# Attention and two feed-forward layers: the late gate written back to PSUM, its split finished by VectorE, a second buffer for two combinations, new scheduler numbers

## Chip, cores and metric

The kernel runs on one core of one Trainium2 chip. The metric is the device time of one execution in microseconds (us); the time of record is the median of several runs.

## What is computed

```python
attn_out = _attn_ref(q, k, v)          # 4 batches, 8 heads, 576 tokens, head 64, mask in blocks of 64
x = attn_out.transpose(0, 2, 1, 3).reshape(B * S, H * D)      # 2304 x 512
h = x @ moe_w_in                       # 512 -> 2048
x = (np.maximum(h, 0) + alpha * np.minimum(h, 0)) @ moe_w_out # layer 0
h = x @ moe2_w_in
out = (h / (1 + np.exp(-1.702 * h))) @ moe2_w_out             # layer 1
```

Inputs of the attention are fp32, the feed-forward weights are float64 and are narrowed to fp32 on the chip. The matmuls are done in fp32r: each operand is split into a high and a low part, and a product is three matmuls (high by high, high by low, low by high).

## The kernel before

**Early stage.** Attention runs over 20 passes (batch, head pair): transposes on TensorE, scores, softmax on ScalarE and VectorE, a DMA transpose of the split probabilities, and the product with v. Beside it, TensorE computes layer 0 for the first 8 of the 16 slices of 128 hidden units: `gemm1` (line 206) multiplies a block of 288 tokens with eight slices, `gate` makes g from it, `gate_split` splits g into the two parts in `gs`, and `g2_half` (lines 249 to 251) multiplies with the output weights and leaves a partial sum in DRAM (`xa`).

**Late stage.** What is left of layer 0 (8 slices) and all of layer 1 (16 slices) is done in 60 *jobs*. A job is two slices for one *unit* of 512 tokens (the last unit of a layer has 256). Its first product uses one level of Strassen's scheme: seven products of combinations of weights (`ws`) and of x (`xc`), in `first_half` (four of them, 24 matmuls of 128x256, or 18 for the small unit) and `second_half` (18, or 6). They go into two PSUM banks, `ga` and `ep`; there are four such banks, so job p + 2 takes the banks of job p. Between the halves `snap` copies parts out (ScalarE, GpSimd), and `sums` adds them in VectorE (lines 786 to 791), after which the two banks hold h of the two slices. Units run in the order 0, 1, 4, 2, 3 for layer 0 and 0 to 4 for layer 1, with four jobs each in layer 0 and eight in layer 1.

Then, for each of the two banks, `gate` (lines 215 to 224) applies the gate: ScalarE reads the bank into an SBUF tile `g` (two buffers), VectorE multiplies `g` with the bank and writes `g` again; the bank is free after that. `gate_split` (lines 226 to 234) copies `g` on ScalarE to the high part `gh` in fp32r, and GpSimd subtracts, `gl = g - gh` (line 127). Both parts lie in `gs`, which has room for two jobs. `g2` (line 813) multiplies them with the output weights into four accumulator banks `acc`, 24 matmuls of 512 columns for a job (12 for layer 1's small unit). After a unit's last job `block_out` drains the accumulators: in layer 0 it loads the partial sum (`o<-xa`, line 822, two `o` buffers), VectorE adds the accumulator (line 823) and a DMA stores it.

Weights of the late stage are loaded as float64 (`rw`), narrowed by ScalarE and three VectorE operations (lines 154 to 160), and then either combined and stored to DRAM (`comb`, `wc<-wc`) or split at once (`split_w`, VectorE and GpSimd in turn, line 127). `load_x` loads a unit's x (`xr`, 1 MB, one buffer) and `comb_x` makes its seven combinations `xc`, each with one buffer.

**The order of the work** is set by a planner that runs while the kernel is built. Each step is announced with `at(kind, n, fn)`; a step's due number is n plus a tenth of `ORDER[kind]` plus `SHIFT[kind]`. `arrange` then simulates the five queues with the durations of `cost` and the dependences, takes on each engine the ready instruction with the smallest due number, and fixes that order. Each engine executes its list strictly in that order.

Of the kernel before, what the change touches and what calls it, by code (L numbers as in the profile page):

```python
# [10 lines left out]
F32R = mybir.dt.float32r  # L11
# [5 lines left out]
ALU = mybir.AluOpType  # L17
# [28 lines left out]
    "split x 2": 8, "load w": 9, "load w 2": 9, "load x": 9, "load k": 9.5, "load q": 9.5, "load v": 9.5, "load alpha": 9.6,  # L46
}
SHIFT = {
    "comb 2": 94.3, "comb 3": -127.7, "first": -19.1, "gate": -18.1, "gate 2": 14.5, "gemm1": -26.2,
    "gemm1 2": 12.5, "gemm2": 168.7, "half": 66.6, "half out": 34.0, "high": 61.0, "load alpha": -77.9,  # L50
    "load k": 64.3, "load q": -45.2, "load v": 58.7, "load w": 60.2, "load w 2": -69.5, "load w 3": -51.5,
    "load wc": -44.3, "load x": -39.6, "narrow": 188.9, "narrow 2": 43.0, "narrow 3": -38.3, "norm": -13.7,
    "out": 35.0, "prep out": 51.5, "prep t": -194.0, "prep v": 152.1, "pv": -88.9, "pv out": 17.0,
    "rest": 55.6, "score": -123.6, "second": 32.2, "setup": 61.8, "snap": -44.3, "soft": -0.0,
    "split g": 101.8, "split g 2": -42.6, "split w": 8.2, "split w 2": 13.0, "split w 3": -12.4,
    "split x": 384.6, "split x 2": 178.0, "sums": 55.9, "warm": 90.0,
}
BIG = 1.0e30

# [2 lines left out]
def kernel(  # L62
# [19 lines left out]
    NA = 8  # L82
# [9 lines left out]
    TH = TB // 2  # L92
    scale = 1.0 / float(D) ** 0.5

    pe, dve, act, pool, sp = nc.tensor, nc.vector, nc.scalar, nc.gpsimd, nc.sync
# [3 lines left out]
    wts_a = ctx.enter_context(tc.tile_pool(name="wts_a", bufs=1))  # L99
    raw = ctx.enter_context(tc.tile_pool(name="raw", bufs=2))  # L100
    blk = ctx.enter_context(tc.tile_pool(name="blk", bufs=1))
# [11 lines left out]
    nalph = const.tile([128, NF], F32, name="nalph")  # L113
# [5 lines left out]
    def at(kind, n, fn):  # L119
        plan.append((n, ORDER[kind], len(plan), fn, n + 0.1 * ORDER[kind] + SHIFT.get(kind, 0)))  # L120


    def hi_part(dst, src, scale_=1.0):
        act.activation(out=dst, in_=src, func=ACTF.Copy, scale=scale_)  # L124

    def lo_part(eng, dst, src, hi):
        eng.tensor_tensor(out=dst, in0=src, in1=hi.bitcast(F32), op=ALU.subtract)  # L127
# [52 lines left out]
    pend = {}  # L180
    late = {}
# [28 lines left out]
    def gbuf(key, name):  # L210
        if key[0] == 0:
            return tmp_p.tile([128, TA], F32, tag="g", name=name)
        return late["x"].tile([128, TB], F32, tag="g", bufs=2, name=name)

    def gate(key, layer, f):
        ps, n = pend[key, f]
        g = gbuf(key, "g")[:, 0:n]
        if layer == 0:
            act.activation(out=g, in_=ps, func=ACTF.Relu, scale=-1.0)
            dve.scalar_tensor_tensor(out=g, in0=g, scalar=nalph[:, f:f + 1], in1=ps, op0=ALU.mult, op1=ALU.add)  # L220
        else:
            act.activation(out=g, in_=ps, func=ACTF.Sigmoid, scale=1.702)
            dve.tensor_tensor(out=g, in0=g, in1=ps, op=ALU.mult)  # L223
        pend[key, f] = (g, n)

    def gate_split(key, f, lo, z=None):
        g, n = pend.pop((key, f))

        w, z = (TA, f % NA) if key[0] == 0 else (TB, z)
        gh, gl = gs_[:, 2 * z * w:2 * z * w + n], gs_[:, (2 * z + 1) * w:(2 * z + 1) * w + n]  # L230
        hi_part(gh, g)
        lo_part(lo, gl, g, gh)
        gt[key, f] = (gh, gl)
# [59 lines left out]
    hl = [[one.tile([128, 128 * g[3]], F16, name=f"hl{j}{x}") for x in range(NHL[j])] for j, g in enumerate(GRP)]  # L293
# [109 lines left out]
    first = []  # L403
# [136 lines left out]
    for u, (i, g, s) in enumerate(slots):  # L540
        n = 2 * u
# [12 lines left out]
    for i in range(len(passes)):  # L554
# [8 lines left out]
        for z, what in enumerate(todo):  # L563
            n = n0 + z * (cnt - (i == N0)) // len(todo)
# [112 lines left out]
    def load_wc(p):  # L677
        l, (_, t0, n, _), j = jobs[p]
        if l == 0 and j in wc0:
            wc[p] = wc0[j]  # L680
            return
        ts = []
        for i in range(7):
            if n == TB or i in (2, 3, 5, 6):
                t = slot(j if l == 0 else (p - P2) % NSL, i)
                sp.dma_start(out=t.bitcast(F32).rearrange("p h c -> p (h c)"), in_=wcs[l][j][i])
            else:
                t = None
            ts.append(t)
        wc[p] = ts  # L690
        if l == 0:
            wc0[j] = ts

    wc0 = {}
    wc = {}
    UO = (0, 1, 4, 2, 3), (0, 1, 2, 3, 4)
    units = [(l, TB * y, min(TB, NT - TB * y), (l + 1, y)) for l in range(2) for y in UO[l]]
    jobs = [(u[0], u, j) for u in units for j in range(NPAIR[u[0]])]
    xc = {}
# [9 lines left out]
    def comb_x(u, i):  # L709
        l, t0, n, key = u  # L710
        r = xb[key]
        b11, b21 = r[:, 0:2, 0:TH], r[:, 2:4, 0:TH]
        if n < TB:
            x = {0: b11, 1: b21}[i]
        else:
            b12, b22 = r[:, 0:2, TH:TB], r[:, 2:4, TH:TB]
            two_ = {0: (b11, b22, ALU.add), 2: (b12, b22, ALU.subtract), 3: (b21, b11, ALU.subtract), 5: (b11, b12, ALU.add),
                    6: (b21, b22, ALU.add)}
            if i in two_:
                x = late["x"].tile([128, 2, TH], F32, tag="xt", bufs=2, name="xt")  # L720
                y, y2, op = two_[i]
                pool.tensor_tensor(out=x, in0=y, in1=y2, op=op)
            else:
                x = b11 if i == 1 else b22
        pl, tag = (blk, ("xlb", "xh0")[i]) if i < 2 else (late["x"], f"xc{i}")
        t = pl.tile([128, 2, 2, TH], F32R, tag=tag, name="xc")
        hi_part(t[:, 0], x)
        lo_part(dve, t[:, 1], x, t[:, 0])
        xc[key, i] = t

    def prod(ps, p, i, y, first, last):
        key = jobs[p][1][3]
        w, x = wc[p][i], xc[key, y]
        z = 0
        for c in range(2):
            sl = slice(128 * c, 128 * c + 128)
            for st_, mv in ((w[:, 0, sl], x[:, 0, c]), (w[:, 0, sl], x[:, 1, c]), (w[:, 1, sl], x[:, 0, c])):
                pe.matmul(ps, st_, mv, start=first and z == 0, stop=last and z == 5, skip_group_check=True)  # L738
                z += 1

# [30 lines left out]
    def second_half(p):  # L771
        g, e = mm[p][:2]
        if jobs[p][1][2] == TB:
            prod(g[:, 0:TH], p, 6, 6, False, False)
            prod(g[:, TH:TB], p, 4, 4, False, True)
            prod(e[:, 0:TH], p, 3, 3, False, True)
        else:
            prod(g[:, 0:TH], p, 6, 1, False, True)
        wc.pop(p)
# [53 lines left out]
    n = n2  # L833
# [6 lines left out]
    for p, (l, u, j) in enumerate(jobs):  # L840
        n, key = place[p], u[3]
        at("load wc", place[max(p - 2, 0)] - 4 * (p < 2), lambda p=p: load_wc(p))
        at("first", n, lambda p=p: first_half(p))
        at("snap", n + 0.3, lambda p=p: snap(p))
        at("second", n + 0.9, lambda p=p: second_half(p))
        at("sums", n + 1.3, lambda p=p: sums(p))
        for y, f in enumerate(fpair(l, j)):
            z = 2 * (p % 2) + y
            at("gate 2", n + 1.4, lambda key=key, l=l, f=f: gate(key, l, f))
            at("split g 2", n + 1.4, lambda key=key, f=f, z=z: gate_split(key, f, pool, z))  # L850
            at("gemm2", place[p + 2] + 0.1 + 0.1 * y, lambda u=u, f=f, a=j == 0 and y == 0, b=j == NPAIR[l] - 1 and y == 1: g2(u, f, a, b))
        if j == NPAIR[l] - 1:
            at("out", place[p + 2] + 0.4, lambda u=u: block_out(u))
    for u in units:
        n = start[u[3]]
# [11 lines left out]
    for y, (n, l, j, f) in enumerate(sorted(seq_w, key=lambda o: o[0])):  # L867
        n = at_w = max(int(n), at_w + 1)
# [74 lines left out]
def cost(eng, kind, ins, outs):  # L943

    n = max(free_size(a) for a in ins + outs)
    psum = any(a.tensor.space == PSUM for a in ins)
    if eng == "PE":
        mv, w = ins[:2]
        cols, load = free_size(outs[0]) * (2 if mv.dtype == F32 else 1), free_size(w)
        rows = list(w.ap)[0][1]  # L950
        time = cols / 2.4 + (13.3 if mv.dtype == F32R else 2.7)
        return time, load / 1.2 + 2.5 if BYTES[w.dtype] == 4 else load / 4.8, cols * rows / 128, mode(w)
    if eng == "Activation":
        return (50 if psum else 93) + n / 1.2 + (187 if len(outs) > 1 else 0),
    full = sum(free_size(a) == n for a in ins)
    if eng == "Pool":
        return (35 + n / 1.2 if not ins else 244 + n / 1.2 if full < 2 else 148 + 2.1 * n),
    if not ins:
        return (40 if outs[0].tensor.space == PSUM else 7) + n / 1.92,
    if psum and len(ins) < 3 or n < 8 or kind == "InstTensorReduce":  # L960
        return (65 if n < 8 else 155) + n / 0.96,
    if full < 2:
        return 64 + n / 1.92,
    return (129 if len(ins) > 2 else 68) + n / 0.96,
# [174 lines left out]
```

## Time and profile before

| | |
|---|---|
| median of 3 runs | 1079.42 us (1077.47 to 1079.83) |
| the profiled execution | 1076.91 us, span of its instructions 1075.1 us |
| TensorE matmul busy, weight load busy | 1003.6 us, 895.2 us |
| VectorE, ScalarE, GpSimd busy | 720.8, 630.2, 521.3 us |
| mean granted TensorE clock | 0.981 of full speed |

The matmuls of a profile are pipelined: a record lasts longer than the distance to the next one, so that busy time is no measure of how near TensorE is to its peak; the distance between starts, and the idle time of the weight loader (PEld), tell more.

### The profile page before, as it was taken

Reading aid. Unit: us, or ns where it says so; the run is one execution under the profiler, and the core shown is the slowest. Engines: PE = TensorE matmul, PEld = TensorE weight load, DVE = VectorE, ACT = ScalarE, POOL = GpSimd, SP = SyncE. Lnnn points to the kernel's source line nnn. Section 1 sums busy time; section 2 is a strip of 40 time slices with the busy share of each in tenths; the row PEclk is TensorE's granted clock in tenths of the full one; section 3 lists DMA queues with packets and bytes.
Section 4 is the critical chain, followed back from the end, with each engine's and each line's share of the span. In section 5 each row is a group of like instructions: output and inputs, shape, how many; then the busy total and the mean of one; then the engine's idle time right before and its main releaser. Section 6 shows DMA issues by size and latency. Waiting matters only on the chain.

```text
span 1075.1 us, 19697 instructions
## 1 busy us (share of the span) xinstructions
PE 1003.6 (93%) x6934; PEld 895.2 (83%) x6934; DVE 720.8 (67%) x1314; ACT 630.2 (59%) x1492; POOL 521.3 (48%) x505
## 2 busy tenths in 40 slices
PE   6777979999999999899997999899999999999998
PEld 3545868889889888899987998788889988989887
DVE  6987999888988875879876878588934324422211
ACT  5777988888888885555544544455434333433332
POOL 3344443433425254578656776555555544434322
PEclk9898989999999999999999999999999999999999
DMA  7899999999998979772645688977585666564340
GB/s 177 203 207 202 193 208 209 207 210 194 227 203 168 197 171 256 263 261 98 224 149 187 194 302 281 306 255 267 169 286 185 221 198 186 187 201 122 118 157 20
DMA packets 308082, 216.92 MB, mean 202 GB/s; under 512 B 219664, under 2 KB 246288, under 8 KB 307984
## 3 DMA queue, kind: packets, MB, share of 16 engines
q1 hardware_dynamic: 307984, 215.67, 73.6%
q8 instruction: 55, 0.90, 0.4%
q14 instruction: 43, 0.35, 0.1%
HBM read 143.27 MB, written 40.89 MB: 171 GB/s over the span
## 4 chain that ended last, share of the span: by engine, by line
PE 59%; DMA 11%; ACT 10%; DVE 7%; issue 3%; POOL 2%; SPq 1%; ACTq 0%; DVEq 0%; POOLq 0%
PE acc L813 20%; PE ga L738 13%; PE ep L738 9%; PE pv L523 4%; PE h L206 4%; ACT e L468 2%; DMA rw<-in_moe_w_out_dram 2%; PE sc L445 2%; PE x L250 2%; PE x L249 2%; PE x L251 2%; ACT hl L488 2%; DMA pt<-hl 2%; DMA wc<-wc 2%; DMA rw<-in_moe_w_in_dram 2%
## 5 line engine op out<-in xcount | busy, mean ns | idle before, releaser
L127 POOL TENSOR_TENSOR gs<-g,gs 128x512 fp32r<-128x512 f32 (+2 forms) x184 | 206.3, 1126 | 242.1 <-ACT gs L124 218.7
L738 PE MATMUL ga<-xc,ws 128*128 128x256 f32 x1368 | 189.2, 284 | 10.9 <-DVE g L223 10.7
L738 PEld LDWEIGHTS ga<-xc,ws 128*128 128x128 f32 x1368 | 178.2, 191 | 21.6 <-DVE g L223 13.9
L813 PE MATMUL acc<-wh,gs 128*128 128x512 f32 x576 | 182.4, 392 | 0.5 <-DVE o L823 0.5
L124 ACT ACTIVATE gs<-g 128x512 fp32r<-128x512 f32 (+2 forms) x184 | 97.8, 536 | 81.9 <-PE acc L813 60.3
L738 PE MATMUL ep<-xc,ws 128*128 128x256 f32 x936 | 134.4, 287 | 2.4 <-DVE g L220 1.5
L738 PEld LDWEIGHTS ep<-xc,ws 128*128 128x128 f32 x936 | 124.9, 194 | 7.2 <-DVE g L220 1.9
L813 PEld LDWEIGHTS acc<-wh,gs 128*128 128x128 f32 x576 | 106.4, 188 | 20.3 <-DVE o L823 0.9
L813 PE MATMUL acc<-wl,gs 128*128 128x512 f32 x288 | 112.7, 391 | 0.0
L523 PE MATMUL pv<-pt,vp 128*128 128x256 f16 (+2 forms) x960 | 92.7, 244 | 9.1 <-DMA pt<-hl 5.5
L813 PE MATMUL acc<-gs,wh 128*128 128x512 f32 (+1 forms) x320 | 94.6, 376 | 4.7 <-DVE o L823 4.6
L498 DVE SCALAR_TENSOR_TENSOR hl<-e,stat,hl 64x64 f16<-64x64 f32 (+4 forms) x160 | 94.9, 623 | 5.1 <-ACT hl L488 2.7
L206 PE MATMUL h<-xh,wh 128*128 128x288 f32 x256 | 80.3, 314 | 11.2 <-DVE g L220 4.4
L488 ACT ACTIVATE hl<-e,stat 64x64 f16<-64x64 f32 (+4 forms) x160 | 79.4, 552 | 10.5 <-DVE stat L478 6.4
L468 ACT ACTIVATE e<-sc,stat 64x64 f32<-64x64 f32 (+4 forms) x160 | 82.9, 520 | 4.2 <-DVE stat L460 3.5
L523 PEld LDWEIGHTS <-vp 128*128 128x128 bf16 x960 | 64.6, 100 | 23.4 <-DMA pt<-hl 9.6
L206 PE MATMUL h<-xlb,wh 128*128 128x288 f32 x256 | 77.9, 304 | 2.5 <-POOL xlb L127 2.4
L249 PE MATMUL x<-gs,wh 128*128 128x288 f32 x256 | 76.6, 303 | 1.0 <-ACT wh L124 0.6
L250 PE MATMUL x<-gs,wh 128*128 128x288 f32 x256 | 76.2, 299 | 0.4 <-POOL gs L127 0.4
L206 PE MATMUL h<-xh,wl 128*128 128x288 f32 x256 | 76.3, 299 | 0.0
L251 PE MATMUL x<-gs,wl 128*128 128x288 f32 x256 | 76.2, 301 | 0.0
L764 POOL TENSOR_TENSOR v<-u,v 128x256 f32<-128x256 f32 x48 | 40.9, 852 | 66.2 <-ACT v L763 66.1
(94 smaller groups left out, 2165.0 us busy)
## 6 DMA issues: line engine op xcount, KB each, us to landing
ws<-wc SPq DMA_DIRECT2D x284, 256.0 KB, 3.8
wc<-wc SPq DMA_DIRECT2D x84, 256.0 KB, 2.6
rw<-in_moe_w_in_dram SPq DMA_DIRECT2D x32, 512.0 KB, 4.7
rw<-in_moe_w_out_dram SPq DMA_DIRECT2D x32, 512.0 KB, 4.3
nat_q<-in_q_dram SPq DMA_DIRECT2D x24, 288.0 KB, 4.3
nat_k<-in_k_dram SPq DMA_DIRECT2D x16, 288.0 KB, 3.9
nat_v<-in_v_dram SPq DMA_DIRECT2D x16, 288.0 KB, 4.2
xa<-xo SPq DMA_DIRECT2D x32, 144.0 KB, 2.8
```

Source lines behind the costliest of these rows:

```text
L124: act.activation(out=dst, in_=src, func=ACTF.Copy, scale=scale_)
L127: eng.tensor_tensor(out=dst, in0=src, in1=hi.bitcast(F32), op=ALU.subtract)
L206: pe.matmul(ps, st_[:, sl], mv[:, c], start=z == 0, stop=z == 3 * KD - 1)
L249: pe.matmul(ps, oh[:, sl], gh, start=f == 0, stop=False)
L250: pe.matmul(ps, oh[:, sl], gl, start=False, stop=False)
L251: pe.matmul(ps, ol[:, sl], gh, start=False, stop=f == NA - 1)
L468: act.activation(out=eo, in_=v[:, h] if len(heads) > 1 else v, func=ACTF.Exp, scale=-1.0, bias=stat[0:m, 0, a:a + 1], accum_out=stat[0:m, ...
L488: act.activation(out=o, in_=e, func=ACTF.Copy, scale=r)
L498: dve.scalar_tensor_tensor(out=hl_part(j, 1, m, nk, h), in0=es[h][0:m, off:off + nk], scalar=stat[0:m, 2, 2 * a + h:2 * a + h + 1], in1=hl ...
L523: pe.matmul(o, l, r, start=z == 0, stop=z == len(ops) - 1)
L738: pe.matmul(ps, st_, mv, start=first and z == 0, stop=last and z == 5, skip_group_check=True)
L813: pe.matmul(ps, a, b_, start=first and z == 0, stop=last and z == 2)
```

## The change

Four edits.

1. In the late stage (`key[0]` is not 0), `gate` writes its result into the PSUM bank in place of `g`. The high part is then copied from the bank by ScalarE, and the low part is subtracted from there by VectorE in place of GpSimd (`split g 2` now names `dve`).
2. For every second unit, combinations 0 and 2 of x get a tile of their own: combination 0 in a tile `xc0`, combination 2 in two tiles that held the weight slice 7 of the early stage. A combination is now handled as a pair of views.
3. `SHIFT` has new numbers for nearly every kind.
4. The planner's cost of a ScalarE operation with SBUF input and a second tensor operand rises from 93 to 186 ns plus the columns.

```diff
 SHIFT = {
-    "comb 2": 94.3, "comb 3": -127.7, "first": -19.1, "gate": -18.1, "gate 2": 14.5, "gemm1": -26.2,
...
+    "comb 2": 35.0, "comb 3": -62.2, "first": 58.5, "gate": -35.3, "gate 2": 49.1, "gemm1": 46.5,
...
     def gate(key, layer, f):
         ps, n = pend[key, f]
         g = gbuf(key, "g")[:, 0:n]
+        to = ps if key[0] else g
         if layer == 0:
             act.activation(out=g, in_=ps, func=ACTF.Relu, scale=-1.0)
-            dve.scalar_tensor_tensor(out=g, in0=g, scalar=nalph[:, f:f + 1], in1=ps, op0=ALU.mult, op1=ALU.add)
+            dve.scalar_tensor_tensor(out=to, in0=g, scalar=nalph[:, f:f + 1], in1=ps, op0=ALU.mult, op1=ALU.add)
         else:
             act.activation(out=g, in_=ps, func=ACTF.Sigmoid, scale=1.702)
-            dve.tensor_tensor(out=g, in0=g, in1=ps, op=ALU.mult)
-        pend[key, f] = (g, n)
+            dve.tensor_tensor(out=to, in0=g, in1=ps, op=ALU.mult)
+        pend[key, f] = (to, n)
...
-        pl, tag = (blk, ("xlb", "xh0")[i]) if i < 2 else (late["x"], f"xc{i}")
-        t = pl.tile([128, 2, 2, TH], F32R, tag=tag, name="xc")
-        hi_part(t[:, 0], x)
-        lo_part(dve, t[:, 1], x, t[:, 0])
+        odd = units.index(u) % 2
+        if i == 2 and odd:
+            t = [wts_a.tile([128, 2, TH], F32R, tag=f"{y}0_{NA - 1}", name="xc") for y in "hl"]
+        else:
+            pl, tag = (blk, ("xlb", "xh0")[i]) if i < 2 and not (odd and i == 0) else (late["x"], f"xc{i}")
+            t = pl.tile([128, 2, 2, TH], F32R, tag=tag, name="xc")
+            t = t[:, 0], t[:, 1]
+        hi_part(t[0], x)
+        lo_part(dve, t[1], x, t[0])
...
-            at("split g 2", n + 1.4, lambda key=key, f=f, z=z: gate_split(key, f, pool, z))
+            at("split g 2", n + 1.4, lambda key=key, f=f, z=z: gate_split(key, f, dve, z))
...
-        return (50 if psum else 93) + n / 1.2 + (187 if len(outs) > 1 else 0),
+        return (50 if psum else 93 if len(ins) < 2 else 186) + n / 1.2 + (187 if len(outs) > 1 else 0),
```

The new numbers move the work. Three places follow.

TensorE in the first jobs of layer 1's second unit. `ga` and `ep` rows are products of jobs (42 to a job), `acc` rows are `g2`. Before:

```order
L813 MATMUL acc<-wh_9498,gs 128x512
L738 MATMUL ga<-xc,ws 128x256 x12
L738 MATMUL ep<-xc,ws 128x256 x12
L738 MATMUL ga<-xc,ws 128x256 x12
L738 MATMUL ep<-xc,ws 128x256 x5
L738 MATMUL ga<-xc,ws 128x256 x12
L738 MATMUL ep<-xc,ws 128x256 x13
L738 MATMUL ga<-xc,ws 128x256 x12
L738 MATMUL ep<-xc,ws 128x256 x6
L813 MATMUL acc<-wh_8260,gs 128x512
```

The same place now:

```order
L819 MATMUL acc<-wh_9501,gs 128x512
L744 MATMUL ga<-xc,ws 128x256 x12
L744 MATMUL ep<-xc,ws 128x256 x6
L744 MATMUL ga<-xc,ws 128x256 x12
L744 MATMUL ep<-xc,ws 128x256 x12
L819 MATMUL acc<-wh_8262,gs 128x512
```

Before, two whole jobs (84 products) stood between two stretches of `g2`, here jobs 30 and 31; now it is the second half of one job and the first half of the next (42), then the 24 matmuls of `g2`, and so on in the same pattern through nearly the whole late stage.

VectorE in the first eight jobs of layer 1, over one job. Lines 157 to 160 narrow a weight tile, `wl` is a weight's low part, 786 to 789 (792 to 795 now) are the sums, 223 (224 now) the gate. Before:

```order
L786 TENSOR_TENSOR u<-ep,v 128x256
L157 TENSOR_SCALAR wa<-sq 128x512
L787 TENSOR_TENSOR u<-u,ga 128x256
L159 SCALAR_TENSOR_TENSOR wa<-sq,wa 128x512
L788 TENSOR_TENSOR ep<-ep,u 128x256
L160 SCALAR_TENSOR_TENSOR sq<-rw,wa 128x512
L157 TENSOR_SCALAR wa<-sq 128x512
L223 TENSOR_TENSOR g<-g,ga 128x512
L159 SCALAR_TENSOR_TENSOR wa<-sq,wa 128x512
L127 TENSOR_TENSOR wl_9119<-sq,wh_9118 128x512
L160 SCALAR_TENSOR_TENSOR sq<-rw,wa 128x512
L223 TENSOR_TENSOR g<-g,ep 128x512
```

Now:

```order
L160 SCALAR_TENSOR_TENSOR sq<-rw,wa 128x512
L793 TENSOR_TENSOR u<-u,ga 128x256
L794 TENSOR_TENSOR ep<-ep,u 128x256
L795 TENSOR_TENSOR ga<-ga,u 128x256
L127 TENSOR_TENSOR wl_9122<-sq,wh_9121 128x512
L157 TENSOR_SCALAR wa<-sq 128x512
L224 TENSOR_TENSOR ga<-g,ga 128x512
L159 SCALAR_TENSOR_TENSOR wa<-sq,wa 128x512
L224 TENSOR_TENSOR ep<-g,ep 128x512
L127 TENSOR_TENSOR gs<-ga,gs 128x512
L160 SCALAR_TENSOR_TENSOR sq<-rw,wa 128x512
L127 TENSOR_TENSOR gs<-ep,gs 128x512
```

The sums stand together, the gate writes `ga` and `ep`, and the two low parts `gs` have come to VectorE.

The DMA queue at the turn from layer 0's unit 4 to unit 2. Before:

```order
L824 DMA x2s<-o 128x512 x2
L822 DMA o<-xa 128x512
L653 DMA wc_4_0_134<-wc 128x512
L704 DMA xr<-xs 128x4x512
L822 DMA o<-xa 128x512
L653 DMA wc_4_1_135<-wc 128x512
```

Now:

```order
L830 DMA x2s<-o 128x512 x2
L828 DMA o<-xa 128x512
L141 DMA rw<-in_moe_w_in_dram 128x4x128
L828 DMA o<-xa 128x512
L654 DMA wc_4_0_134<-wc 128x512
L141 DMA rw<-in_moe_w_in_dram 128x4x128
L654 DMA wc_4_1_135<-wc 128x512
L830 DMA x2s<-o 128x512 x2
L654 DMA wc_4_2_136<-wc 128x512
L828 DMA o<-xa 128x256
L654 DMA wc_4_3_137<-wc 128x512
L705 DMA xr<-xs 128x4x512
```

The 1 MB load of the next x (`xr`) stood between the third and the fourth partial sum of the unit that is drained; now it follows both, and a weight load of 512 KB stands between them.

## Rows read from the trace of the kernel before

**Rows 1.** The page, part 1: busy time, share of the span, instructions.
```profile
PE 1003.6 (93%) x6934; PEld 895.2 (83%) x6934; DVE 720.8 (67%) x1314; ACT 630.2 (59%) x1492; POOL 521.3 (48%) x505
```
**Rows 2.** Busy time by stretch: us, then each engine, granted clock, DMA share, GB/s.
```profile
0.00:200.00 200.00, 162.46 (x1181) 128.76 (x1182) 169.47 (x342) 157.55 (x413) 80.44 (x82) 0.93 0.95 202
...
455.00:690.00 235.00, 226.46 (x1496) 208.32 (x1495) 179.62 (x274) 119.72 (x250) 163.73 (x157) 0.99 0.65 217
690.00:790.00 100.00, 91.52 (x546) 80.37 (x545) 75.65 (x109) 48.89 (x90) 57.27 (x48) 0.98 0.76 258
```
**Rows 3.** The same view in stretches of 25 us, those with a lowered clock.
```profile
575.00:600.00 25.00, 20.39 (x157) 20.09 (x156) 14.90 (x25) 10.04 (x23) 16.00 (x19) 0.93 0.46 156
...
675.00:700.00 25.00, 21.79 (x132) 19.28 (x132) 13.91 (x30) 11.78 (x24) 14.51 (x17) 0.93 0.86 284
...
775.00:800.00 25.00, 23.10 (x162) 21.98 (x161) 10.72 (x26) 10.08 (x19) 11.94 (x13) 0.93 0.97 340
```
**Rows 4.** The chain that ended last: start, us, what.
```profile
840.48 2.88 PE ga L738 x24
...
845.51 5.47 PE acc L813 x24
...
870.92 0.64 ACT gs L124
...
871.63 1.30 POOL gs L127
...
1058.84 12.73 PE acc L813 x56
```
**Rows 5.** Waits of the weight loader, 650 to 800 us: total, times, longest.
```profile
PEld ga L738 <- DVE g L223: 12.2, 7, 2.3
...
PEld ep L738 <- DVE g L220: 0.7, 1, 0.7
```
**Rows 6.** The same, 455 to 650 us.
```profile
PEld acc L813 <- DVE o L823: 4.8, 1, 4.8
PEld ep L738 <- DVE g L220: 1.2, 1, 1.2
```
**Rows 7.** The same, 400 to 455 us.
```profile
PEld h L206 <- DVE g L220: 2.4, 1, 2.4
```
**Rows 8.** The same, 800 to 1075 us.
```profile
PEld ga L738 <- DVE g L223: 1.8, 3, 1.4
```
**Rows 9.** Timeline around 755 us: start, us, engine, line, operation.
```profile
751.66 1.29 POOL L127 TENSOR_TENSOR gs<-g,gs 128x512 fp32r<-128x512 f32 x1 [2.99 <-ACT gs L124]
751.77 1.73 DVE L159 SCALAR_TENSOR_TENSOR wa<-sq,wa 128x512 int32<-128x512 int32 x1
...
755.45 0.41 DVE L789 TENSOR_TENSOR ga<-ga,u 128x256 f32<-128x256 f32 x1
...
755.89 0.69 DVE L127 TENSOR_TENSOR wl<-sq,wh 128x512 fp32r<-128x512 f32 x1
...
756.59 0.69 DVE L223 TENSOR_TENSOR g<-g,ga 128x512 f32<-128x512 f32 x1
```
**Rows 10.** Groups by line, 690 to 775 us: busy, mean ns, idle before.
```profile
L159 DVE SCALAR_TENSOR_TENSOR wa<-sq,wa 128x512 int32<-128x512 int32 x13 | 16.3, 1254 | 0.0
L127 POOL TENSOR_TENSOR gs<-g,gs 128x512 fp32r<-128x512 f32 x14 | 20.5, 1474 | 16.1 <-ACT gs L124 16.1
L154 ACT ACTIVATE sq<-rw 128x512 f32<-128x512 f32 x13 | 8.5, 663 | 14.0 <-DMA rw<-in_moe_w_out_dram 14.0
```
**Rows 11.** Timeline at the turn of a unit.
```profile
570.77 0.37 SPq L704 DMA_DIRECT2D xr<-xs  x1
571.23 0.64 SPq L822 DMA_DIRECT2D o<-xa  x1
...
580.55 0.69 DVE L823 TENSOR_TENSOR o<-acc,o 128x512 f32<-128x512 f32 x1 [3.97 <-DMA o<-xa]
```
**Rows 12.** Waits over the whole span.
```profile
ACT g L222 <- POOL gs L127: 69.3, 54, 2.5
```

More of the change, by code (lines that the diff above doesn't have):

```diff
@@ L48 @@
 SHIFT = {
-    "comb 2": 94.3, "comb 3": -127.7, "first": -19.1, "gate": -18.1, "gate 2": 14.5, "gemm1": -26.2,
[L50 to L56, printed above, removed]
+    "comb 2": 35.0, "comb 3": -62.2, "first": 58.5, "gate": -35.3, "gate 2": 49.1, "gemm1": 46.5,
+    "gemm1 2": 12.5, "gemm2": 59.1, "half": 110.6, "half out": -22.5, "high": 19.0, "load alpha": -0.4,
+    "load k": 9.7, "load q": -168.0, "load v": -25.2, "load w": 61.9, "load w 2": 11.9, "load w 3": 3.0,
+    "load wc": -24.2, "load x": -20.5, "narrow": 297.4, "narrow 2": 65.6, "narrow 3": 20.9, "norm": 13.4,
+    "out": 4.8, "prep out": 20.2, "prep t": -7.1, "prep v": 81.6, "pv": 5.9, "pv out": 23.1, "rest": 20.2,
+    "score": -5.4, "second": 58.6, "setup": -9.8, "snap": -57.0, "soft": -4.0, "split g": 64.1,
+    "split g 2": -56.1, "split w": -8.4, "split w 2": 13.3, "split w 3": -3.0, "split x": 56.6,
+    "split x 2": 192.1, "sums": -166.0, "warm": 67.8,
 }
@@ L736, in prod @@
             sl = slice(128 * c, 128 * c + 128)
-            for st_, mv in ((w[:, 0, sl], x[:, 0, c]), (w[:, 0, sl], x[:, 1, c]), (w[:, 1, sl], x[:, 0, c])):
+            for st_, mv in ((w[:, 0, sl], x[0][:, c]), (w[:, 0, sl], x[1][:, c]), (w[:, 1, sl], x[0][:, c])):
                 pe.matmul(ps, st_, mv, start=first and z == 0, stop=last and z == 5, skip_group_check=True)
```

## The prediction

> **What bounds the kernel now.** I read the totals first, then busy time by stretch, the chain, the waits of the weight loader, and last the timeline at the worst waits. The totals say TensorE: 1003.6 us of 1075.1 with a matmul running, no other engine above 67% [rows 1]. The matmuls are the same 6934 after the change, so time can only come from the distance between them. Where nothing holds it, TensorE goes at a fixed pace: 24 products in 2.88 us (0.12 each), 24 matmuls of the second layer in 5.47 us (0.228 each) [rows 4]. So I look for what TensorE loses. In the first 200 us it is busy for only 162 of them, but there the DMA engines are at 0.95 [rows 2]. The change adds no work there and the order of TensorE's list is nearly the same, so this part is not where I expect a result. In the late stage the loss is in few places:
>
> - After 650 us the weight loader waits 12.2 us in 7 waits for the gate's multiplication, the one that frees a product bank, and 0.7 us for the same thing in layer 0 [rows 5].
> - At the turn of a unit it waits 4.8 us once for VectorE's drain of an accumulator, and 1.2 us for a gate [rows 6].
> - Before the late stage it waits 2.4 us for an early gate [rows 7], and after 800 us only 1.8 us in three waits [rows 8].
> - Three stretches of 25 us have a mean granted clock of 0.93 [rows 3]. Each follows one of these waits, and 7% of 25 us is about 1.75 us of work lost.
>
> **Why the gate is late.** ScalarE waits 69.3 us in all, in 54 waits, for GpSimd's low part before it may overwrite `g` [rows 12], and its list is stuck for that time. In the chain GpSimd's low part takes 1.30 us after a high part of 0.64 [rows 4]. VectorE, which must do the gate, has in 690 to 790 us 75.65 us of work [rows 2], but part of it is stretched: the narrowing operation of line 159 took 1.73 us when it began just behind a low part of GpSimd, while a VectorE subtraction of the same size with both inputs in SBUF took 0.69 a little later [rows 9]. The mean of line 159 there is 1.254 us [rows 10].
>
> **The change part by part.**
>
> *Low part to VectorE.* GpSimd loses 120 operations of about 1.3 us; VectorE gains 120 with one operand in PSUM. The nearest row is the gate's multiplication, also one PSUM and one SBUF operand of 512 columns: 0.69 us [rows 9]. In 690 to 775 us that is 14 x 0.69 = 9.7 us more for VectorE [rows 10]. Against it, what GpSimd's low parts stretched goes: line 159 alone has 13 x (1.254 - 0.69) = 7.3 us of stretch, and line 160 is alike. GpSimd keeps other work, so I count half of about 15 us. VectorE's load so rises by about 2 us in 100: the cover is a VectorE that stays below 80% busy. If the stretch stays, it is 85%.
>
> The Trainium skill ("VectorE: DVE Perf Modes", Rules for kernel authors) says that matmul output which is worked on several times should be copied from PSUM to SBUF first, and its errata section gives a PSUM source 62 cycles more at 0.96 GHz, about 0.065 us as an estimate, which would make the 28 gate and split operations of that stretch 1.8 us dearer; the rows show 0.69 us with PSUM and 0.69 us without [rows 9], so I give it no price.
>
> *The bank is held longer.* It is now free after the low part, not after the multiplication: one more ScalarE copy (0.64 [rows 4]) and one more subtraction (0.69), with hand-overs about 1.5 us. Who waits for it is the first half of the job after next. Here the new order matters. Before, jobs 30 and 31 stood together, which left 6 matmuls of the second layer and 42 products between a job's end and the reuse of its bank: 1.4 + 5.0 = 6.4 us. Now 24 and 42 stand there: 10.5 us, almost everywhere. The chain to be covered is four sums of 0.41, sigmoid, multiplication, copy and subtraction of about 0.65 to 0.69 each, and one more 0.69 for the second bank: 5.0 us with nothing else in VectorE's list. In layer 1's first eight jobs two weight tiles are narrowed per job, six operations and a low part in the same list: 7 x 0.69 makes 9.8 us, still covered. So I let 10 of the 12.9 + 2 x 1.75 = 16.4 us of gate waits and slow clock go (bounds: none, all). What is late next there is the narrowed weight: ScalarE already waits 14.0 us for the float64 loads [rows 10], which nothing in the change shortens.
>
> *DMA order at the unit turn.* The 1 MB load was issued at 570.77, the partial sum right behind it at 571.23, and its adder ran only at 580.55, after 3.97 us of idle VectorE [rows 11]; that is the 4.8 us wait. Now the two partial sums go first, with one 512 KB weight load between. I take 6 of 4.8 + 1.2 + 1.75 = 7.75 us off (bounds: none, all).
>
> *Early end and steady part.* The last early blocks are put in another order on TensorE, which may or may not keep their one wait [rows 7]: 1.5 of 2.4 us (0 to 2.4). After 800 us: 1 of 1.8 us.
>
> *Two combinations with a second buffer.* They lift a wait of ScalarE and GpSimd at ten unit turns. The previous unit's products of combinations 0 and 2 come first in its last job, some 9 us before the next unit begins, so that wait is hidden and the edit is worth nothing by itself; without that cover it would cost one copy and one subtraction per turn, 1.3 us.
>
> *New costs.* The last 56 matmuls of the second layer hid all of the last gates, 12.73 us [rows 4]; now 24 stand behind the last product, 12 of them (2.7 us) in front of the ones that need the last gate, whose chain is about 2.4 us for 256 columns: 0.5 us (0 to 1.5). VectorE's more crowded list in 455 to 690 us, where it has 179.6 of 235 us [rows 2] and gets 42 low parts, 27 us at most: +3 us for new short waits (0 to 10). The planner's numbers and the ScalarE cost line also move things in the attention stage, by a few places: 0, between -6 and +6.
>
> **Sum.** -10 - 6 - 1.5 - 1 + 0.5 + 3 = -15 us. The profiled execution took 1076.9 us, 2.5 below the median of 1079.4; against the median this gives 1064 us.
>
> **Rivals.**
>
> - *The bank becomes the bound (slower).* If VectorE's narrowing operations stay at 1.25 us, the covered chain in layer 1's first eight jobs is 5.0 + 6 x 1.25 + 0.7 = 13 us, over the 10.5 that the order leaves. That is the point from which it decides. Then each of the 8 + 1 + 3 gate waits after 455 us [rows 5, 6, 8] grows by the 1.5 us of longer holding: +18, less 6.5 for the unit turn: 1091 us. For it: 0.93 clocks show how thin the cover is; against it: the operation that stretched them leaves GpSimd. Chance 0.10.
> - *The stretch after 650 us is bound by its loads.* The DMA share is 0.86 in 675 to 700 us [rows 3], ScalarE waits for float64 words, and the gate sits behind them in ScalarE's list. Then the 10 us stay, the rest comes: 1074 us. Chance 0.20.
> - *Everything late goes.* All waits and slow clocks, 16.4 + 7.75 + 2.4 + 1.8 = 28 us, and no new ones: 1051 us, and below if the attention stage gains too. Chance 0.10.
> - *Nothing moves.* The new numbers move the 1 MB load and the waits elsewhere at the same price (the turn's and the gates' waits stay, 2.5 gained, 3.5 lost): 1080 us. Chance 0.08.
>
> **Chances and range.** The forecast, with 1056 to 1071 us around it, keeps 0.52. A measurement of this kernel tells about 0.2% (2.2 us) from no change. Faster: 0.52 + 0.20 + 0.10 = 0.82; within: 0.08; slower: 0.10. The range goes from 1050 to 1078 us: below it is half of the case in which everything goes, above it the slower case and part of no change.
>
> **What would show it.** Right: ScalarE's wait for GpSimd's low part (69.3 us) is gone; the low part runs on VectorE in about 0.69 us; line 159's mean falls below 1.0 us; the waits of `ga` for VectorE after 650 us fall from 12.2 us to some 4, now named by the low part; the accumulator wait of 4.8 us is gone and with it one slow clock. Wrong: `ga` waits for the low part more than 12 us in all, or the time up to the first late product (about 455 us) differs by more than 6 us: then the attention stage, which I leave out, decides.

## The result and the profile after

The changed kernel takes 1063.54 us (median of 4 runs, 1060.99 to 1065.77) against 1079.09 us before (4 runs): ratio 0.9857, 95% interval 0.9829 to 0.9885. That is 15.6 us less; 1064 us was forecast. The profiled execution took 1065.77 us, the slowest of the four, so that the two traces differ by only 11.1 us (1076.91 to 1065.77), and the accounts below are made against that.

The totals of the page, and busy time by stretch (us, then PE, PEld, DVE, ACT, POOL with their counts, granted clock, DMA share, GB/s):

```profile
PE 994.3 (93%) x6934; PEld 892.6 (84%) x6934; DVE 739.2 (69%) x1434; ACT 614.7 (58%) x1492; POOL 368.0 (35%) x385
```

```profile
0.00:200.00 200.00, 157.91 (x1156) 125.24 (x1157) 164.77 (x337) 154.40 (x403) 80.67 (x80) 0.91 0.93 197
200.00:400.00 200.00, 190.92 (x1614) 177.53 (x1613) 173.00 (x373) 172.64 (x488) 81.41 (x89) 1.00 0.96 206
...
455.00:690.00 235.00, 229.32 (x1511) 211.12 (x1510) 179.71 (x328) 120.22 (x256) 111.22 (x118) 0.99 0.67 222
690.00:790.00 100.00, 94.59 (x583) 84.05 (x583) 75.58 (x129) 48.37 (x93) 31.80 (x31) 1.00 0.79 263
```

GpSimd has lost 153 us and VectorE gained only 18 [rows 1], though it now runs 120 more operations. In 690 to 790 us VectorE's load is the same as before, 75.6 against 75.65 us [rows 2], with 20 more operations in it, and TensorE gets 583 matmuls into the 100 us where it got 546. In the first 200 us TensorE is busy 4.6 us less than before, at a lower mean granted clock (0.91 against 0.93 [rows 2]).

Where the early stage ends is told better by the first `g2` matmul of the late stage: it starts at 484.5 us, before at 484.9, now with 108 products done ahead of it in place of 126. At 0.12 us each [rows 4] these 18 are 2.2 us, so the front is some 1.8 us behind. From that matmul to the end of the span it was 590.2 us and is now 579.5: nearly all of the gain lies in the late stage.

The waits of the weight loader, 455 to 650 us and 650 to 800 us (total, times, longest); after 800 us there is none left where there were 1.8 us [rows 8]:

```profile
PEld acc L819 <- DVE o L829: 4.2, 1, 4.2
PEld ep L744 <- DVE gs L127: 0.7, 1, 0.7
PEld ga L744 <- DVE gs L127: 0.3, 1, 0.3
...
PEld ep L744 <- DVE gs L127: 2.9, 2, 2.5
PEld acc L819 <- ACT wh L124: 2.7, 1, 2.7
PEld acc L819 <- DVE o L829: 1.5, 2, 0.9
PEld acc L819 <- ACT gs L124: 1.0, 1, 1.0
PEld acc L819 <- ACT o L832: 0.9, 2, 0.5
PEld ga L744 <- DVE gs L127: 0.5, 1, 0.5
```

The 12.9 us for the gate after 650 us [rows 5] have become 3.4 us, and their releaser is now the low part `gs`, the last reader of the bank. In their place stands 2.7 us for a weight that is not yet split. The wait for an accumulator, 4.8 us [rows 6], is still there with 4.2 us, but at another place. The DMA queue and VectorE around it (start, us, engine, line, operation):

```profile
634.18 0.38 SPq L830 DMA_DIRECT2D x2s<-o  x1
...
636.85 0.42 SPq L828 DMA_DIRECT2D o<-xa  x1
...
640.70 0.32 SPq L828 DMA_DIRECT2D o<-xa  x1
...
642.01 0.69 DVE L829 TENSOR_TENSOR o<-acc,o 128x512 f32<-128x512 f32 x1 [1.41 <-DMA o<-xa]
```

This is the turn from unit 2 to unit 3. The rows are the store of the second partial sum, the loads of the third and the fourth, and the adder of the third. There are two `o` tiles, so the third and fourth partial sums can only be loaded when the first two have been stored. The store of the first landed at 632.87, but the load of the third was issued only at 636.85, behind weight transfers and the second's store, and landed at 641.99. Its adder ran at 642.01, and that ends TensorE's wait. No large load stands between the third and the fourth now; the fourth was issued at 640.70 and added at 647.39, and TensorE had no such wait for it.

### The profile page after: what moved, and what is told of

The parts are those of the page before. It is cut to its first block, busy times and chain, and to the rows that moved or that the text cites. A ratio compares the mean times of both kernels' runs of the same rounds, so it can differ in the third digit from the quotient of the medians.

```text
span 1064.0 us, 19650 instructions
## 1 busy us (share of the span) xinstructions
PE 994.3 (93%) x6934; PEld 892.6 (84%) x6934; DVE 739.2 (69%) x1434; ACT 614.7 (58%) x1492; POOL 368.0 (35%) x385
## 4 chain that ended last, share of the span: by engine, by line
PE 57%; DMA 7%; ACT 3%; DVE 3%; issue 3%; POOL 1%; SPq 0%; ACTq 0%; DVEq 0%; POOLq 0%
PE acc L819 24%; PE ga L744 13%; PE ep L744 9%; PE h L206 4%; DMA rw<-in_moe_w_out_dram 2%; PE pv L524 2%; DMA pt<-hl 2%; PE x L251 1%; PE x L250 1%; PE x L252 1%; DMA wc<-wc 1%; DMA xa<-xo 1%; DMA o<-xa 1%; DMA x2s<-o 1%; PE sc L446 1%
## 5 line engine op out<-in xcount | busy, mean ns | idle before, releaser
L819 PE MATMUL acc<-wh,gs 128*128 128x512 f32 x576 | 186.1, 391 | 4.3 <-ACT wh L124 2.5
L744 PE MATMUL ga<-xc,ws 128*128 128x256 f32 x1368 | 184.4, 283 | 0.2
L744 PE MATMUL ep<-xc,ws 128*128 128x256 f32 x936 | 131.8, 283 | 2.6 <-DVE gs L127 2.6
L744 PEld LDWEIGHTS ep<-xc,ws 128*128 128x128 f32 x936 | 121.1, 192 | 4.0 <-DVE gs L127 3.6
L770 POOL TENSOR_TENSOR v<-u,v 128x256 f32<-128x256 f32 x48 | 38.6, 805 | 214.3 <-ACT v L769 214.3
L768 ACT ACTIVATE u<-ga 128x512 f32<-128x512 f32 x48 | 28.5, 593 | 139.3 <-PE ga L744 139.2
L499 DVE SCALAR_TENSOR_TENSOR hl<-e,stat,hl 64x64 f16<-64x64 f32 (+4 forms) x160 | 90.7, 605 | 4.6 <-ACT hl L489 4.1
L792 DVE TENSOR_TENSOR u<-ep,v 128x256 f32<-128x256 f32 x48 | 20.2, 421 | 101.8 <-PE ep L744 101.8
L127 POOL TENSOR_TENSOR gs<-g,gs 128x288 fp32r<-128x288 f32 x64 | 61.2, 963 | 83.6 <-ACT gs L124 77.3
L250 PE MATMUL x<-gs,wh 128*128 128x288 f32 x256 | 75.8, 301 | 1.0 <-DVE g L221 0.4
```

The lines of the kernel that those rows point to most:

```text
L250: pe.matmul(ps, oh[:, sl], gh, start=f == 0, stop=False)
L499: dve.scalar_tensor_tensor(out=hl_part(j, 1, m, nk, h), in0=es[h][0:m, off:off + nk], scalar=stat[0:m, 2, 2 * a + h:2 * a + h + 1], in1=hl ...
L768: act.activation(out=u, in_=g, func=ACTF.Copy)
L770: pool.tensor_tensor(out=v, in0=u[:, TH:TB], in1=v, op=ALU.subtract)
L819: pe.matmul(ps, a, b_, start=first and z == 0, stop=last and z == 2)
```

## The experiments

For each, the ratio is to the kernel before in the same session. The kernel before had medians of 1077.11 to 1080.33 us in these sessions, so kernels of different sessions are compared by their ratios; the change has 0.9857 (0.9829 to 0.9885). Where a difference is small, the text also gives the time from the first `g2` matmul of the late stage to the end in the profiled executions (590.2 us before, 579.5 with the change), one execution of each kernel.

### The table alone, and the gate alone

The first takes the kernel before and gives it the new `SHIFT` and the new ScalarE cost. The second gives it the new gate and nothing else:

```diff
+        to = ps if key[0] else g
...
-            at("split g 2", n + 1.4, lambda key=key, f=f, z=z: gate_split(key, f, pool, z))
+            at("split g 2", n + 1.4, lambda key=key, f=f, z=z: gate_split(key, f, dve, z))
```

> The kernel before with the new SHIFT table and the new ScalarE cost alone: gate, GpSimd's low part and the single buffers stay. If the gain is the order that the table sets, about 1066 us and the waits of ga for the gate after 650 us fall below 5 us. If the gain is GpSimd losing the low part, no gain: 1077 to 1085 us, with the 69 us of ScalarE waiting for GpSimd still there and the gate's waits near 12 us. If both are needed together, slower than before, up to 1090 us.

> The kernel before with the gate written to PSUM and the low part on VectorE alone: old table, old cost, single buffers. If GpSimd's low part was the cause, about 1066 us. If the order is what counts, 1077 us or more. If the bank's longer holding costs anything where the table does not leave room for it, slower than before: 1080 to 1090 us, with ga waiting for gs on VectorE.

Measured: the table alone 1084.92 us (1.0042, interval 1.0015 to 1.0069), slower than before. The gate alone 1074.78 us (0.9944, 0.9912 to 0.9975). The gate's edit is thus worth 5.6 us without any new numbers, and the numbers are worth less than nothing without it. Where the table's kernel loses, 650 to 800 us:

```profile
ACT sq L154 <- DMA rw<-in_moe_w_out_dram: 15.8, 7, 4.2
DVE wa L157 <- ACT sq L154: 14.8, 8, 4.9
PEld acc L813 <- ACT wh L124: 14.0, 4, 7.4
```

The waits for layer 1's gate are down to 1.9 us over the whole late stage, but the second layer waits 14 us for split weights, whose narrowing waits for its loads. The kernel with the gate alone shows the wait that the slower rival described, a product bank held until the low part is done (425 us to the end):

```profile
PEld ga L739 <- DVE gs L127: 8.5, 7, 3.2
PEld acc L814 <- DVE o L824: 4.7, 3, 2.0
PEld ga L739 <- ACT u L763: 3.6, 3, 2.6
```

So that wait exists where the order does not leave room. It takes the place of the old one and is smaller: from 425 us to the end all waits for a bank behind its gate come to 10.2 us here, with 1.7 for `ep`, where they came to 18.3 in the kernel before. That fits the gain; no run isolates it.

### The bank's hold and VectorE's operand, with the order fixed

Since any edit makes the planner write a new order, this one has the lists of the changed kernel written into it, and only moves the gate's result back to the tile `g`:

```diff
-        to = ps if key[0] else g
+        to = g
```

> The changed kernel with the order of every engine fixed to its own, and the gate's result kept in the SBUF tile g (two buffers) in place of the PSUM bank; the low part stays on VectorE, now with two SBUF inputs. If the longer holding of the bank costs, this is 1 to 4 us faster. If what the bank buys is that ScalarE no longer waits for g, this is 3 to 10 us slower, with a wait of ScalarE's gate for VectorE's low part. If neither matters, within 2 us, and VectorE's low part is stretched above 0.69 us only where GpSimd runs.

Measured: 1065.62 us (0.9858, 0.9810 to 0.9906), no difference to the change that can be told in the total. The low part on VectorE over the late stage, first of this kernel, then of the change (busy, mean ns, idle before):

```profile
L127 DVE TENSOR_TENSOR gs<-g,gs 128x512 fp32r<-128x512 f32 x96 | 85.3, 911 | 9.2 <-ACT gs L124 6.7
```

```profile
L127 DVE TENSOR_TENSOR gs<-ga,gs 128x512 fp32r<-128x512 f32 x48 | 32.9, 686 | 2.2 <-ACT gs L124 0.6
L127 DVE TENSOR_TENSOR gs<-ep,gs 128x512 fp32r<-128x512 f32 x48 | 32.7, 681 | 4.0 <-ACT gs L124 3.8
```

With both inputs in SBUF the same subtraction takes 0.911 us on average, with one in PSUM 0.68. The 96 operations cost 19.7 us more of VectorE. The stretch is there only where GpSimd runs, as expected: in this kernel the 22 that met no GpSimd operation took at most 0.70 us, the 74 others 0.98 on average and up to 1.79; with the operand in PSUM none of the 96 took more than 0.69, though GpSimd ran beside 73 of them.

The edit moves two things at once, and the waits of the weight loader show them pulling against each other (425 us to the end, first of this kernel, then of the change):

```profile
PEld acc L819 <- DVE o L829: 9.7, 7, 4.3
```

```profile
PEld acc L819 <- DVE o L829: 5.7, 3, 4.2
PEld ep L744 <- DVE gs L127: 3.6, 3, 2.5
```

The waits for a bank behind its gate fall from 4.4 to 1.2 us, and the waits for VectorE's adder rise by 4.0. The time from the first `g2` matmul to the end is 582.4 us against 579.5. So neither the longer hold of the bank nor VectorE's operand is shown to be free; what is shown is that the two together leave the total where it was, within its interval.

### Four places for the partial sums

With the order fixed, a unit of layer 0 has four places for its partial sums (two of them in space that the early stage leaves), and in the DMA queue the third and fourth load follow the second directly, for the units after the first:

```diff
-            o = late["x"].tile([128, DM], F32, tag="o", bufs=2, name="o")
+            if l or d < 2:
+                o = late["x"].tile([128, DM], F32, tag="o", bufs=2, name="o")
+            elif d == 2:
+                o = blk.tile([128, 2 * TA], F32, tag="gs7", name="o")[:, 0:DM]
+            else:
+                o = wts_a.tile([128, DM], F32, tag=f"l1_{NA - 1}", name="o")
```

> The changed kernel with its own order fixed, four places for the partial sums of a unit in place of two (two of them in space that the early stage leaves), and in the DMA queue the third and fourth load moved right behind the second, for units after the first. If the unit turn's stall is the reload of these two, the accumulator waits of 4.2 and 1.5 us and one slow clock go: 5 to 7 us faster than the change, about 1057 us. If TensorE then waits for the next thing in the same place, no more than 2 us.

Measured: 1060.43 us (0.9810, 0.9762 to 0.9857). By the medians that is 3.1 us under the change, by the ratios some 5, where 5 to 7 were expected; the two intervals overlap. The time from the first `g2` matmul to the end is 577.3 us, 2.2 less than with the change. The accumulator still waits 2.9 us at this turn, for VectorE's adder:

```profile
PEld acc L823 <- DVE o L838: 2.9, 2, 2.5
```

Of 5.7 us of such waits 2.8 are gone. The adder of the third partial sum no longer waits for a load: it runs at 638.85, right behind a low part. With the fixed lists it still stands where it stood for the late load.

> The changed kernel with four places for a unit's partial sums and the planner free to make the order anew with the same numbers. With the order fixed this gave 1060.4 us. If the numbers carry over to a slightly different program, 1058 to 1062 us. If they fit only the program they were made for, as the old ScalarE cost suggests (1077 us), 1066 to 1078 us.

With the same four places and the planner free: 1057.97 us (0.9815, 0.9791 to 0.9838). The stretch of this turn, as a window of the trace:

```profile
625.00:650.00 25.00, 25.00 (x151) 22.27 (x151) 16.73 (x31) 12.40 (x26) 9.65 (x13) 1.00 0.89 299
```

TensorE is busy all of it, at full clock; the change had 21.03 of 25 us there at a granted clock of 0.93. No wait for an adder of `o` is left in the late stage. The next wait is for a bank and ends at 656 us, with a lowered clock behind it (0.86 in 650 to 675 us):

```profile
PEld ep L748 <- DVE gs L127: 2.6, 1, 2.6
```

From the first `g2` matmul to the end it is 573.0 us, 6.5 less than with the change. This kernel has the lowest median of all; by the ratio it is level with the fixed order (0.9815 and 0.9810), and its interval just overlaps that of the change.

### The second buffers

Without them (`odd = 0`), the planner makes a new order with the same numbers:

> The changed kernel without the second buffers of the two combinations; the planner makes a new order with the same numbers. If they are worth nothing by themselves, as predicted, 1062 to 1067 us. If the even order of the late stage rests on them (the change's own order cannot be executed without them), 1070 us or more, with waits at the unit turns on ga for xc or on the accumulators.

Measured: 1068.25 us (0.9890, 0.9848 to 0.9932), 4.7 us more than the change by the medians and 3.6 by the ratios, between the two outcomes that were expected. The intervals overlap, but from the first `g2` matmul to the end it is 585.6 us, 6.1 more than with the change. Is it the buffers, or the order? The next kernel has the second buffers, but the order of the kernel without them, written in:

> The changed kernel, second buffers and all, with the order fixed that the planner made without them (the 1068.25 us kernel's). If the buffers' own cover is worth nothing and only the order that they allow counts, 1067 to 1069 us. If the buffers themselves save waits at the unit turns, 1063 to 1065 us.

Measured: 1069.40 us (0.9918, 0.9887 to 0.9950), 584.7 us from the first `g2` matmul to the end. With the buffers and the other's order it is as slow as without the buffers, and it has the same waits, first in the kernel without buffers, then in this one (425 us to the end; the change has 0.8 and 1.0):

```profile
PEld ga L744 <- DVE gs L127: 6.1, 6, 3.0
PEld acc L819 <- ACT gs L124: 5.3, 2, 4.3
```

```profile
PEld ga L744 <- DVE gs L127: 6.1, 5, 3.2
PEld acc L819 <- ACT gs L124: 5.7, 2, 4.5
```

So under this order the buffers themselves gain nothing. What they give is the order that the planner writes when it has them.

### The other edits undone

The changed kernel with gate and low part as before, everything else kept:

> The changed kernel with gate and low part as before (SBUF tile, GpSimd); table, cost line and second buffers stay. The table alone gave 1084.9 us, with accumulators waiting 14 us for split weights. If the move of the low part is what clears those, this stays at 1080 us or above; if the second buffers did it, 1066 us.

Measured: 1086.31 us (1.0051, 1.0024 to 1.0079). The second buffers do not help the table either; without the gate's edit it is slower than before.

The changed kernel with the planner's old ScalarE cost, not one operation different:

```diff
-        return (50 if psum else 93 if len(ins) < 2 else 186) + n / 1.2 + (187 if len(outs) > 1 else 0),
+        return (50 if psum else 93) + n / 1.2 + (187 if len(outs) > 1 else 0),
```

> The changed kernel with the old ScalarE cost in the planner: no computing changes, but every list is made anew. If the numbers are robust, within 4 us of 1064. If the table fits only the cost it was made with, 1068 to 1080 us: then a part of the gain is the fit of one order and belongs to no edit.

Measured: 1077.25 us (0.9988, 0.9963 to 1.0012). Some 14 us hang on 93 ns in the planner's model of a ScalarE operation with SBUF input and a scale from SBUF, as `high` in the softmax has it. Its stretches:

```profile
0.00:200.00 200.00, 162.11 (x1171) 129.69 (x1172) 169.92 (x330) 152.19 (x395) 82.89 (x85) 0.91 0.90 193
200.00:400.00 200.00, 182.58 (x1488) 166.38 (x1487) 169.63 (x363) 166.13 (x472) 72.05 (x74) 0.96 0.96 202
```

In 200 to 400 us, TensorE runs 1488 matmuls where the change runs 1614. The first `g2` matmul starts at 502.9 us, 18.4 later than in the change, and from there to the end it is 576.2 us, 3.3 less. So the loss lies in the attention stage, in no one wait: the waits for the softmax in 200 to 300 us come to 4.7 us in nine, against 2.0 in the change.

### The early gate and the partial sum

Two experiments with the order fixed, on the wait at 450 us, 2.7 us in the change: ScalarE's gate there waits until a partial sum `xo`, which shares the two tiles `g`, has been stored. First, `xo` gets one tile of its own:

```diff
-            return tmp_p.tile([128, TA], F32, tag="g", name=name)
+            return tmp_p.tile([128, TA], F32, tag=name, bufs=2 if name == "g" else 1, name=name)
```

> The changed kernel with its order fixed; the early stage's partial sums xo get one buffer of their own, so that the early gate need not wait until a partial sum has left the tile g. If the 2.7 us wait at 450 us is that DMA, it goes, and the slow clock behind it: 3 to 4 us faster, about 1060. If xo with one buffer waits for itself, no gain or 2 us slower.

Measured: 1079.03 us (1.0001, 0.9978 to 1.0025), a clear miss: 15.5 us slower than the change, where 3 to 4 faster were expected. The one tile waits for its own store, over the whole span:

```profile
ACT xo L256 <- DMA xa<-xo: 28.3, 11, 4.4
```

Then three tiles for both (`bufs=3`, the same space):

> The changed kernel with its order fixed and three buffers, in place of two, for the early tile that the gate's g and the partial sum xo share. If the wait at 450 us (ScalarE's gate behind the store of xo) is the shared ring, 2.7 us and a slow clock of 1.75 us go: 1059 to 1061 us, and the wait of the early gate for the store (6.7 us in the same kernel's trace with g in SBUF) falls under 2 us. If the store only shows up one step later, within 1.5 us of 1063.5.

Measured: 1062.43 us (0.9866, 0.9843 to 0.9888), no difference to the change that can be told. The wait of the gate for the store falls from 7.9 us to 1.9, as expected, but TensorE's wait stays:

```profile
PEld h L206 <- DVE g L221: 2.9, 2, 2.3
```

The store is thus not all of it. The longer of the two waits ends at 449.08 us, and its gate stands in ScalarE's list behind a weight that is being narrowed, which waits for its load:

```profile
447.49 0.66 ACT L154 ACTIVATE sq<-rw 128x512 f32<-128x512 f32 x1 [1.88 <-DMA rw<-in_moe_w_in_dram]
```

No run moved this load.

## Why the prediction was right

The total came out within 0.5 us of the median, and that is in part luck: the largest term, the gate waits, held, the second largest failed by 4 to 5 us, smaller ones that came out better made up for part of it, and the four runs lie 4.8 us apart. Neither sign of being wrong came: `ga` waits 0.8 us for the low part, not more than 12, and the first late product starts at 467.2 us where it started at 465.4, 1.9 us later and not more than 6 ("about 455 us" was too early for it). Point by point, against the profiled executions:

- **The low part leaves GpSimd (right).** The wait of ScalarE for GpSimd's late low part, 69.3 us [rows 12], is gone. The low part takes 0.68 us where 0.69 was taken. Line 159 fell from 1.254 us [rows 10] to 0.941 us, line 160 from 1.241 to 0.750, which is 10.4 us off for both where half of 15 was counted, and VectorE's load in 690 to 790 us did not rise at all, where 2 us were forecast. The row of line 159:

```profile
L159 DVE SCALAR_TENSOR_TENSOR wa<-sq,wa 128x512 int32<-128x512 int32 x13 | 12.2, 941 | 0.1
```

- **Gate waits after 650 us, -10 (right).** 12.9 us became 3.4, and the two slow clocks there are gone: 13 us together (9.5 and 3.5). Against them stand 2.7 us for weights, 1.0 for a high part and 0.9 for an output tile, so some 8.4 us net. That the narrowed weight would be "late next there" is what the trace shows.
- **DMA order at the unit turn, -6 (wrong).** The step that failed is "Now the two partial sums go first". They do at that turn, and it has no accumulator wait any more. But the turn from unit 2 to unit 3 got one of 4.2 us, for the third partial sum, and the slow clock behind it, so between 1 and 2 us were gained. I had taken the 1 MB load as the cause, and it was one way to be late; the standing cause is two tiles for four partial sums, with a reload in between. With four places and the order fixed, 2.8 of the 5.7 us of waits for the adder went, and all of them when the planner could use the places.
- **Early end, -1.5 (wrong, small).** 2.4 us [rows 7] are 2.7 now.
- **After 800 us, -1 (right, larger).** 1.8 us became none.
- **New short waits, +3, and the end, +0.5 (too dear).** In 455 to 650 us the waits for `gs` are 1.0 us; behind the last product the 24 matmuls of the second layer run without a gap, as the chain shows:

```profile
1053.80 0.71 PE ga L744 x6
1054.52 5.48 PE acc L819 x24
```

- **Attention stage, 0 within 6 (size inside, reach misjudged).** The front is some 1.8 us behind, inside the bound. Executions differ by more: with the same lists in this stage, the two kernels with fixed order, `g` in SBUF and four places, start their first `g2` matmul at 480.4 and 482.9 us, where the change does at 484.5. But the old ScalarE cost shows that the same table can lose far more there: over 18 us of the front, some 14 in all.
- **Second buffers, "worth nothing by itself" (right for the buffers, wrong for the edit).** The two runs show both halves: no gain from the buffers under the other order, and some 4 to 6 us from the order that rests on them. The prediction looked for the wait that a buffer removes and did not ask which order it makes possible.
- **The slower rival.** Its mechanism is real: with the gate alone `ga` waits 8.5 us for `gs`. Under the change's order it is small, 0.8 us for `ga` and 3.6 for `ep`; that the 10.5 us between a job and the reuse of its bank cover it is argued. The tile in place of the bank, in the same order, took 3.2 us off these waits and was no faster in all.

In sum, for the two profiled executions: all waits of the weight loader from 455 to 800 us, the small ones with them, come to 23.3 us before and 14.7 after, and of three slow clocks of 1.75 us one is left: -12.1. After 800 us it is 3.1 before and none now. The front is 1.8 us behind. That makes -13.4 where the traces differ by 11.1 us; the 2 us between are open.

## What to carry to other kernels

Where a planner writes the lists, an edit is worth what the new lists are worth: here the gate's edit was worth 5.6 us alone, the new numbers cost 4.6 alone, and a buffer that gains nothing under another order gave some 4 to 6 by allowing its own. Take edits apart twice, once with the planner free and once with the order written in; only the second tells what the edit itself does, and only if it moves one thing. When totals agree, compare the stages too: two effects can cancel. And when a stall is traced to one late transfer, ask first how many tiles the transfer has: moving the transfer moves the stall.

## What the runs showed of the hardware

A VectorE subtraction of 128x512 in fp32 that reads one operand from PSUM was not stretched by GpSimd in this kernel: 0.68 us on average over 96 operations and 0.69 at most. The same with both operands in SBUF took 0.911 us on average in the same order, and up to 1.79 beside GpSimd. The Trainium skill ("SBUF — State Buffer", SBUF: two separate sides) describes an exclusive port that GpSimd and a VectorE operation with two SBUF inputs contend for; both traces agree with it: with two SBUF inputs 0.98 us where GpSimd ran beside the operation and 0.68 where it did not, with one 0.68 in either case. So for VectorE a result that is read again is, in this kernel, no worse off in PSUM than in SBUF; its bank is held longer for it.
